# Attention and token/channel mixer in one kernel: load order of the last channel weight, score banks for batch 1's attention products, GpSimd casts of the token weights, and the planner's picking rules

## The chip, the cores and the metric

The kernel runs on one core of one Trainium2 chip. The metric is the device time of one execution in microseconds. Each number given as "the time" is a median over several executions; the profile is one further execution, recorded by the hardware profiler. The core has five instruction queues that matter here: PE (TensorE matrix products), DVE (VectorE), ACT (ScalarE), POOL (GpSimd) and SP (SyncE, which issues every DMA of this kernel). Each works through its own list in order and waits at its head for semaphores.

## What is computed

Eight batches of causal attention with a decay along the sequence, then a mixer: a token product over the sequence and a channel product over the features. Cut to what matters:

```python
batch, n_heads, seq, head_dim = (8, 8, 576, 64)       # d_model 512
d_tok, d_ch = (256, 1536)
...
cum = np.cumsum(np.maximum(s, 0.0), axis=-1)
bias = -(cum[:, :, :, None] - cum[:, :, None, :])
scores = np.where(causal, -1000000000.0, scale * q @ kT + np.minimum(bias, 0.0))
attn = softmax(scores)
x = (attn @ v).transpose(0, 2, 1, 3).reshape(B, S, H * D)
...
xt = x.transpose(0, 2, 1)
h = np.maximum(xt @ w_tok1, 0.0) @ w_tok2
u = x + h.transpose(0, 2, 1)
return u + np.maximum(u @ w_ch1, 0.0) @ w_ch2
```

Inputs and output are float32; the products run in bfloat16 with float32 sums.

## The kernel before

**Work of one batch.** The heads of a batch go in two groups of four (`quad(b, 0)` and `quad(b, 4)`). `stage_qk` loads k and q of four heads (576 KB each), casts them to bfloat16 (`qkb`, L657 on GpSimd, L659 on VectorE, L661 on ScalarE) and VectorE transposes them (L668, `kT` and `qT`). `stage_v` loads v in five chunks and multiplies it with the decay weights (L618, `vp`). `quad` makes scores in two phases (L700, for batches 0 and 1 with a mask product L709), exponentials on ScalarE (L716, tile `E`), for later batches a causal mask on GpSimd (L723), then one set of nine attention products for each head (L740, "AV" below); VectorE takes the reciprocal of the row sums (L749) and normalizes into `x` (L754). `tok` is the token mixer: L964 and L972 (first token weight `w1`), `h` evicted with a relu (L978 ACT, L979 DVE), L989 and L993 (second token weight `w2`), the sum with `x` (L1006), a transpose into `uTa` or `uTb` (by L1019 on TensorE with evictions L1027 and L1029 for batches 0 and 1, by a transposing DMA, L1011, from batch 2 on). `chan` is the channel mixer: L1047 with channel weight 1, relu evictions into `ga` or `gb` (L1053 ACT, L1055 DVE), then L1073 with channel weight 2, the sum L1081 and the store. Batch 0 has its own form of both, `tok0` (L860 with `w1`, L873, L879 with `w2`, evictions L885 and L886) and `chan0` (L902 with channel weight 1, L924 with channel weight 2, L928, copies L935, stores L940).

**PSUM.** There are eight banks: four in the ring `r_sc` (score banks, `psc` in the profile) and four in `r_mx` (mixer banks, `pmx`). Scores of all batches but the first's second phase use `r_sc`. The AV products use `r_mx`, except those of the first four heads of batch 0; so do all products of `tok`, `chan` and `chan0`.

**Weights.** `load_tok1`, `load_tok2` and `load_ch1`, `load_ch2` load the weights in float32 into tiles that are not in use yet (`uTb`, `x`, `ga`, `vf`) and cast them to bfloat16 with `load_w`, whose last argument names the engines that may do the cast (L783 GpSimd, L785 VectorE, L787 ScalarE). Channel weights 1 and 2 come in four groups each (0 to 3) of 768 KB.

**The order of work.** Nothing is written out by hand. Each piece of work is an `Op` with the engines that could do it (and an assumed time on each), what it reads and writes, which ring slots it holds and a priority. `Plan.once` goes through time in a model: for each engine it lists the ops that could start (`cands`), takes those within 0.03 us of the earliest, and picks among them by the longest remaining path (`tail`, from `Plan.tails`) on VectorE, ScalarE and GpSimd, or by priority on TensorE and SP. It may then prefer an op that starts later than the picked one, if that shortens the longer of the two remaining paths; the later op may start as late as the picked one would have ended. An op that another engine could finish sooner is passed over. `Plan.run` repeats this and keeps the shortest plan; the resulting order on each engine is what is emitted. So an edit of one load or one bank can change the order on all engines for the rest of the run. Loads stand in SP's queue in the order of the calls at the end of the kernel (L1095 to L1123): `load_op` chains each load to the one before.

Two more details: the load of k or q needs a free slot of four in `qkf`, which is free when the tile has been cast and, from batch 2 on, squared by ScalarE (L643, a check of the value range). And where TensorE would be idle in the first 45 us of the plan, products of zeros (L1185) are filled in.

Of the kernel before, what the change touches and what calls it, by code (L numbers as in the profile page):

```python
# [49 lines left out]
class Plan:  # L50
# [8 lines left out]
        self.writer = {}  # L59
        self.readers = {}  # L60

    def op(self, alts, reads=(), writes=(), prio=0, dma=0.0, holds=(), after=None, port=False):
        o = Op()
        o.port = port
        o.alts = alts
        o.prio = prio
        o.dma = dma
        o.idx = len(self.ops)
        o.deps = set()
        o.users = []  # L70
        o.bufs = []
        for k in list(reads) + list(writes) + list(holds):
            b = k[0] if isinstance(k, tuple) else k
            if isinstance(b, Buf) and b not in o.bufs:
                o.bufs.append(b)
                b.uses += 1
        for k in reads:
            w = self.writer.get(k)
            if w is not None:
                o.deps.add(w)  # L80
        for k in writes:
            w = self.writer.get(k)
            if w is not None:
                o.deps.add(w)
            for r in self.readers.get(k, ()):
                o.deps.add(r)
        for k in reads:
            self.readers.setdefault(k, []).append(o)
        for k in writes:
            self.writer[k] = o  # L90
            self.readers[k] = []
        o.deps.discard(o)
        o.after = after
        if after is not None:
            o.deps.add(after)
        self.ops.append(o)
        return o
# [12 lines left out]
    def tails(self, order):  # L110
        nxt = {}
        last = {}
        for o in reversed(order):
            nxt[o] = last.get(o.eng)
            last[o.eng] = o
        follow = {}
        for r in {b.ring for o in order for b in o.bufs}:
            prev = {}
            for b in r.uses:
                if b.slot in prev:  # L120
                    for o in prev[b.slot].ops:
                        follow.setdefault(o, []).append(b.ops[0])
                prev[b.slot] = b
        for o in sorted(order, key=lambda o: (-o.start, -o.idx)):
            t = o.fin - o.start
            for u in follow.get(o, ()):
                t = max(t, o.fin - o.start + u.tail)
            for u in o.users:
                t = max(t, self.gap(o, u, o.eng) + u.tail)
            n = nxt[o]  # L130
            if n is not None and o.eng in ("PE", "SP"):
                t = max(t, o.alts[o.eng][0] + n.tail)
            o.tail = t

    def reset(self):
        rings = set()
# [42 lines left out]
    def once(self, use, eps=0.03):  # L179
# [14 lines left out]
        port = 0.0  # L194
# [18 lines left out]
        while left:  # L213
            best = None
            for e in engines:
                lst = []
                tmin = None
                for o in cands[e]:
                    st = slot_time(o)
                    if st is None:  # L220
                        continue
                    est = max(etime[e], o.ready, st)
                    if e == "POOL" or o.port and e == "DVE":
                        est = max(est, port)
                    if use and any(max(etime[x], o.ready, st) + o.alts[x][1] < est + o.alts[e][1] - 0.05
                                   for x in o.alts if x != e):
                        continue
                    lst.append((est, o))
                    if tmin is None or est < tmin:
                        tmin = est  # L230
                if tmin is None:
                    continue
                pick = None
                if use and e in ("DVE", "ACT", "POOL"):
                    for est, o in lst:
                        if est <= tmin + eps:
                            key = (-o.tail, o.idx)
                            if pick is None or key < pick[0]:
                                pick = (key, est, o)
                    for est, o in lst:  # L240
                        _, ep, p = pick
                        if o is p or est > ep + p.alts[e][0]:
                            continue
                        if max(est + o.tail, est + o.alts[e][0] + p.tail) + 0.01 < max(ep + p.tail, ep + p.alts[e][0] + o.tail):
                            pick = (None, est, o)
                else:
                    for est, o in lst:
                        if est <= tmin + eps:
# [191 lines left out]
def kernel(  # L440
# [29 lines left out]
    HQ = 4  # L470
# [94 lines left out]
    def decay():  # L565
        P.op(act(576, lambda: nc.scalar.activation(out=s_sb[:, :], in_=s_sb[:, :], func=AF.Relu)),
             reads=["s"], writes=["sr"], prio=-1)
        P.op({"DVE": (1.3, 1.6, lambda: nc.vector.tensor_tensor_scan(
            out=cum[:, :], data0=one_sb[:, :].to_broadcast([64, S]), data1=s_sb[:, :], initial=0.0, op0=ALU.mult, op1=ALU.add))},
            reads=["sr"], writes=["cum"], prio=-1)  # L570
        P.op(dve(1, lambda: nc.vector.tensor_scalar(
            out=half[:, :], in0=cum[:, S - 1 : S], scalar1=-0.5, scalar2=None, op0=ALU.mult)),
            reads=["cum"], writes=["half"], prio=-1)
        P.op(act(576, lambda: nc.scalar.activation(
            out=wn[:, 0:S], in_=cum[:, :], func=AF.Exp, bias=half[:, 0:1], scale=1.0), True),
            reads=["half", "cum"], writes=["wn"], prio=-1)
        bw = Buf(r_sc, False)

        def w_tr():
            for jc in range(NJ):  # L580
                nc.tensor.transpose(out=bw.t[:, jc * 64 : jc * 64 + 64], in_=wn[:, jc * 128 : jc * 128 + 128],
                                    identity=identf[:, :])
        P.op({"PE": (0.7, 1.1, w_tr)}, reads=["wn"], writes=[(bw, 0)], prio=(0,))
        P.op(dve(320, lambda: nc.vector.tensor_copy(
            out=wT[:, :, :].rearrange("p c e -> p (c e)"), in_=bw.t[:, 0:320])),
            reads=[(bw, 0)], writes=["wT"], prio=-1)
# [92 lines left out]
            square(f, b, h, i)  # L679

    xbuf = {}

    def quad(b, h):
        np_ = (b * H + h) / 2
# [2 lines left out]
        for ph, blocks in enumerate(PHASES):  # L687
# [26 lines left out]
            for e in range(HQ):  # L714
                def ex(p=ps[e], e=e, ph=ph):
                    nc.scalar.activation(out=E.t[:, e, ph * 512 : ph * 512 + 512], in_=p.t[:, :], func=AF.Exp, scale=0.125)  # L716
                P.op(act(512, ex), reads=[(ps[e], 0)], writes=[(E, ph, e)], prio=0)
            if pem:
                continue
            for (jc, a, z) in blocks:  # L720
# [8 lines left out]
        x, vp = xbuf[b], vbuf[b]  # L729
        vkeys = [(vp, c) for c in range(NJ)] + [(vp, "w")]  # L730
        for hh in range(HQ):
            pa, rc = Buf(r_sc if b == 0 and h == 0 else r_mx, False), Buf(r_rc, False)

            def av(pa=pa, hh=hh):
                o = pa.t[:, 0 : NJ * 66].rearrange("p (c n) -> p c n", n=66)
                for ic in range(NJ):
                    j_lo = max(ic - 1, 0)
                    for jc in range(j_lo, ic + 1):
                        d0 = EB[jc] + 128 * (ic - jc)
                        nc.tensor.matmul(out=o[:, ic, 0 : D + 1], lhsT=E.t[:, hh, d0 : d0 + 128],  # L740
                                         rhs=vp.t[:, jc, h + hh, 0 : D + 1], start=(jc == j_lo), stop=(jc == ic))
            P.op({"PE": (9 * 0.035, 9 * 0.035 + 0.3, av)},
                 reads=([(E, ph, hh) for ph in range(2)] if pem else
                        [(E, "m", jc) for jc in range(NJ)]) + vkeys, writes=[(pa, 0)],
                 holds=[x, rc], prio=(np_ if b else -1 + h / 8, 0))
# [48 lines left out]
    def load_tok1(buf):  # L794
        def d1(st):
# [3 lines left out]
        load_w(buf, 0, 5 * DT, d1, lambda st: [  # L799
            [(w1[:, 0:2, :].rearrange("p c n -> p (c n)"), st[:, 0 : 2 * DT])],  # L800
            [(w1[:, 2:4, :].rearrange("p c n -> p (c n)"), st[:, 2 * DT : 4 * DT]),
             (w1[0:64, 4, :], st[0:64, 4 * DT : 5 * DT])]], [("w1", 0), ("w1", 1)], 2.5, ("POOL", "DVE"))
        P.op({"POOL": (0.3, 0.5, lambda: nc.gpsimd.tensor_copy(out=w1[64:128, NJ - 1, 128:256], in_=w1[0:64, NJ - 1, 128:256]))},
             reads=[("w1", 1)], writes=["w1s"], prio=30)

    def load_tok2(buf):
        def d2(st):
            nc.sync.dma_start(out=st.rearrange("p (c n) -> p c n", c=NTC),
                              in_=moe_w_tok2.rearrange("(c p) n -> p c n", p=128))
        load_w(buf, 0, NTC * S, d2, lambda st: [[(w2[:, :, :].rearrange("p c n -> p (c n)"), st)]], ["w2"], 1.5,  # L810
               ("POOL", "DVE"))

    NG = 4
    CG = NCC // NG
# [72 lines left out]
                     reads=[(pt, 1)], writes=[(uT, m, a)], prio=0)  # L887
        return uT

    def chan0(uT):  # L890
        rank = 4 + LAG
        g = Buf(r_gb)
        for c0 in range(0, NCC, CG):
            pms = [Buf(r_mx, False) for _ in range(CG)]
            ms = [[m] for m in range(NMC)] if c0 == 0 else [list(range(NMC))]
            for ml in ms:
                for i in range(CG):
                    cc, pm = c0 + i, pms[i]

                    def mm(cc=cc, pm=pm, ml=ml):  # L900
                        for m in ml:
# [4 lines left out]
                         reads=[(uT, m, a) for m in ml for a in (0, NQ // 2)] +  # L906
                               ([("wc1", 0, m // 2) for m in ml] if c0 == 0 else [("wc1", cc // CG)]) +
                               ([(pm, 0)] if ml[0] else []),
                         writes=[(pm, 0)], holds=[g], prio=(rank + 2.0 * c0 / NCC - 4 * (c0 == 0), 3 + ml[0]))
            for i in range(CG):  # L910
                cc, pm = c0 + i, pms[i]
                P.op(either(512,
# [186 lines left out]
    stage_v(0)  # L1099
    for h in range(0, H, HQ):  # L1100
        quad(0, h)
    load_tok1(Buf(r_uTb))
    load_tok2(Buf(r_x))
    sga, sv = Buf(r_ga), Buf(r_vf)
# [3 lines left out]
    load_ch1(sga, 0, 3)  # L1108
    stage_qk(1, 0)
    load_ch2(sga, 1536, 0)  # L1110
    load_ch2(sv, 0, 1)
    load_ch2(sga, 0, 2)
    load_ch2(sga, 1536, 3)
    stage_qk(1, HQ)
    stage_v(1)
    for b in range(2, B):
        for h in range(0, H, HQ):
            stage_qk(b, h)
# [5 lines left out]
    for b in range(B):  # L1124
# [3 lines left out]
        if b:  # L1128
            chan(b, *tok(b))
        else:  # L1130
            chan0(tok0())

    P.op({"DVE": (1.3, 1.6, lambda: nc.vector.tensor_tensor_scan(
        out=pre[:, :], data0=one_sb[:, :].to_broadcast([64, S]), data1=wn[:, 0:S], initial=0.0, op0=ALU.mult, op1=ALU.add))},
# [99 lines left out]
```

## Time and profile before

| what | value |
|---|---|
| time, median of 6 executions | 297.37 us (296.5 to 298.45) |
| time of the profiled execution | 299.43 us |
| span of the profiled execution | 297.7 us |
| PE busy | 282.8 us, 95% of the span |
| ACT busy | 190.0 us, 64% |
| DVE busy | 169.3 us, 57% |
| POOL busy | 88.3 us, 30% |
| DMA, share of 16 engines, SP's queue | 64.5% |
| granted TensorE clock, mean | 0.989 |

The span is the time from the first to the last instruction in the trace; the execution's own time is a little longer. In the slices of the span each digit is the busy share of 1/40 of it in tenths (9 is 90% or more), and the row PEclk is the clock that TensorE was granted, in tenths of full speed. A line of the list of waits names the waiting engine with tile and line, who released it, the sum in us, how often, and the longest. A line in order of time gives start, length, engine, line, operation, tiles written and read, sizes, how many instructions, and in brackets the idle time before it and what ended it. A row of windows gives the stretch, its length, the busy time of the five engines (matrix products and weight loads of TensorE apart) with the count of instructions, the granted clock, the share of the DMA engines and GB/s.

### The profile page before, as it was taken

What the parts mean: (1) busy time and instruction counts of PE and PEld (TensorE: products, weight loads), DVE (VectorE), ACT (ScalarE), POOL (GpSimd) and SP (SyncE); (2) the same over time, 40 slices, a digit from 0 to 9 for tenths busy, and PEclk for the clock granted to TensorE, in tenths of its full rate; (3) what the DMA queues carried; (4) which work ended last, traced back from release to release, by engine and by line L of the source; (5) the groups of instructions that cost most, each with busy time, mean ns of one, the idle gap of its engine ahead of it and who ended that gap; (6) DMA issues with size and microseconds to landing.
All of it is one profiled execution on the core that took longest, in us unless ns stands there. A gap on an engine that the chain in (4) does not pass through costs nothing.

```text
span 297.7 us, 6653 instructions
## 1 busy us (share of the span) xinstructions
PE 282.8 (95%) x2596; PEld 156.7 (53%) x2596; DVE 169.3 (57%) x326; ACT 190.0 (64%) x359; POOL 88.3 (30%) x133
## 2 busy tenths in 40 slices
PE   8789999688979989999999999999999999999994
PEld 3465455536655534545774545446754545447643
DVE  3984846769686757487644745396425533440022
ACT  3784957669879947856888649985883245107600
POOL 3325002567565503263272213731201301000000
PEclk9999999959999999999999999999999999999999
DMA  7999999998988994976890666756002410151023
GB/s 230 272 343 334 375 309 259 203 353 233 325 188 276 263 218 187 206 184 156 279 203 17 142 250 240 235 111 205 2 0 52 127 73 0 46 116 70 2 72 110
DMA packets 68050, 54.09 MB, mean 182 GB/s; under 512 B 53680, under 2 KB 56560, under 8 KB 68016
## 3 DMA queue, kind: packets, MB, share of 16 engines
q1 hardware_dynamic: 68016, 53.64, 64.5%
q8 instruction: 21, 0.34, 0.5%
q14 instruction: 13, 0.11, 0.1%
HBM read 40.65 MB, written 9.44 MB: 168 GB/s over the span
## 4 chain that ended last, share of the span: by engine, by line
PE 66%; DMA 20%; SPq 6%; DVE 3%; POOL 2%; ACT 1%; issue 1%; DVEq 0%; ACTq 0%; POOLq 0%
PE pmx L1073 26%; PE pmx L1047 24%; DMA qkf<-in_q_dram 10%; DMA ga<-in_moe_w_ch_dram 6%; PE psc L700 4%; PE pmx L740 4%; PE pmx L964 4%; PE pmx L989 4%; SPq L611 3%; DMA vf<-in_v_dram 3%; SPq L638 1%; DMA uTa<-ua 1%; DVE x L754 1%; POOL vp L618 1%; PE pmx L972 1%
## 5 line engine op out<-in xcount | busy, mean ns | idle before, releaser
L716 ACT ACTIVATE E<-psc 128x512 bf16<-128x512 f32 x120 | 63.3, 602 | 22.4 <-PE psc L700 16.9
L1047 PEld LDWEIGHTS <-wc 128*128 128x128 bf16 x528 | 50.7, 98 | 35.0 <-issue 4.7
L723 POOL TENSOR_SCALAR_AFFINE_SELECT E<-E 128x512 bf16<-128x512 bf16 (+1 forms) x60 | 35.1, 615 | 91.9 <-ACT E L716 74.9
L1047 PE MATMUL pmx<-uTb,wc 128*128 128x320 bf16 x384 | 54.0, 299 | 1.8 <-DVE gb L1055 1.5
L1073 PE MATMUL pmx<-wc,gb 128*128 128x512 bf16 (+1 forms) x252 | 54.2, 369 | 0.0
L1053 ACT ACTIVATE gb<-pmx 128x320 bf16<-128x320 f32 x83 | 36.3, 438 | 25.0 <-PE pmx L1047 17.9
L643 ACT ACTIVATE junk<-qkf 128x1152 bf16<-128x1152 f32 x32 | 37.5, 1171 | 10.4 <-DMA qkf<-in_k_dram 8.4
L618 POOL TENSOR_TENSOR vp<-vf,wT 128x512 bf16<-128x512 f32 (+1 forms) x31 | 32.1, 1061 | 17.1 <-PE pmx L740 13.3
L1073 PEld LDWEIGHTS <-gb 128*128 128x128 bf16 x252 | 23.7, 98 | 25.3 <-issue 0.7
L1047 PE MATMUL pmx<-uTa,wc 128*128 128x512 bf16 x144 | 32.6, 379 | 1.3 <-DMA uTa<-ua 1.2
L1073 PE MATMUL pmx<-wc,ga 128*128 128x512 bf16 x144 | 32.6, 379 | 0.0
L754 DVE TENSOR_TENSOR x<-pmx,rc 128x320 bf16<-128x320 f32 x60 | 29.1, 490 | 1.8
L1053 ACT ACTIVATE ga<-pmx 128x512 bf16<-128x512 f32 x29 | 16.9, 603 | 13.1 <-PE pmx L1047 13.1
L740 PEld LDWEIGHTS <-E 128*128 128x128 bf16 x576 | 20.5, 97 | 6.6 <-issue 2.7
L1081 DVE TENSOR_TENSOR of<-pmx,ub 128x512 f32<-128x512 f32 (+1 forms) x17 | 11.2, 661 | 20.6 <-PE pmx L1073 18.7
L668 DVE STREAM_TRANSPOSE kT<-qkb 128x576 f32<-128x576 f32 x16 | 20.0, 1252 | 4.0 <-PE psc L700 3.7
L700 PE MATMUL psc<-qT,kT 32*128 32x256 bf16 (+2 forms) x592 | 19.7, 256 | 2.7 <-DVE rc L749 1.4
L740 PE MATMUL pmx<-vp,E 128*128 128x65 bf16 x540 | 21.3, 193 | 1.0 <-DVE x L754 0.8
L1073 PEld LDWEIGHTS <-ga 128*128 128x128 bf16 x144 | 13.4, 98 | 16.1 <-issue 1.1
L657 POOL CAST qkb<-qkf 128x1152 bf16<-128x1152 f32 (+1 forms) x10 | 10.1, 1010 | 38.0 <-DMA qkf<-in_q_dram 19.6
L700 PEld LDWEIGHTS <-kT 32*128 32x128 bf16 x640 | 13.8, 94 | 12.2 <-issue 9.2
L668 DVE STREAM_TRANSPOSE qT<-qkb 128x576 f32<-128x576 f32 x16 | 19.9, 1243 | 0.3 <-POOL qkb L657 0.3
(109 smaller groups left out, 281.1 us busy)
## 6 DMA issues: line engine op xcount, KB each, us to landing
qkf<-in_k_dram SPq DMA_DIRECT2D x20, 576.0 KB, 5.7
qkf<-in_q_dram SPq DMA_DIRECT2D x20, 576.0 KB, 5.3
vf<-in_v_dram SPq DMA_DIRECT2D x32, 256.0 KB, 6.2
out_dram<-of SPq DMA_DIRECT2D x31, 256.0 KB, 2.4
ga<-in_moe_w_ch_dram SPq DMA_DIRECT2D x6, 768.0 KB, 7.8
vf<-in_moe_w_ch_dram SPq DMA_DIRECT2D x2, 768.0 KB, 9.4
out_dram<-of SPq DMA_DIRECT2D x10, 128.0 KB, 2.7
vf<-in_v_dram SPq DMA_DIRECT2D x8, 128.0 KB, 5.1
```

What stands on the lines that cost most here:

```text
L618: eng.tensor_tensor(out=vp.t[0:n, c, :, 0:D], in0=vf.t[0:n, c, :, :], in1=wT[0:n, c, b * H : b * H + H].unsqueeze(2).to_broadcast([n, H, D ...
L643: P.op({"ACT": (1.1, 1.5, lambda: nc.scalar.activation(out=junk[:, :], in_=f.t[:, :], func=AF.Square, accum_out=sq[:, col : col + 1]))}, r ...
L668: nc.vector.transpose(out=T.t[:, 0:S, :].rearrange("p s q -> p (s q)").bitcast(FP32).rearrange("p (t r) -> p r t", r=R), in_=t1.t[:, :].bi ...
L700: nc.tensor.matmul(out=ps[e].t[:, c0 : c0 + z - a], lhsT=kT.t[p0 : p0 + TP, jc * 128 : jc * 128 + 128, qq], rhs=qT.t[p0 : p0 + TP, a:z, qq ...
L716: nc.scalar.activation(out=E.t[:, e, ph * 512 : ph * 512 + 512], in_=p.t[:, :], func=AF.Exp, scale=0.125)
L723: nc.gpsimd.affine_select(out=w, in_=w, compare_op=ALU.is_ge, fill=0.0, base=0, pattern=[[0, HQ], [1, n]], channel_multiplier=-1)
L740: nc.tensor.matmul(out=o[:, ic, 0 : D + 1], lhsT=E.t[:, hh, d0 : d0 + 128], rhs=vp.t[:, jc, h + hh, 0 : D + 1], start=(jc == j_lo), stop=( ...
L754: nc.vector.tensor_tensor(out=x.t[:, :, (h + hh) * D : (h + hh + 1) * D], in0=o[:, :, 0:D], in1=rc.t[:, :].unsqueeze(2).to_broadcast([128, ...
L964: nc.tensor.matmul(out=pms[t].t[:, :], lhsT=w(0, 128, c, t), rhs=x.t[:, c, :], start=(c == 0), stop=False)
L1047: nc.tensor.matmul(out=pm.t[:, 0 : e - a], lhsT=wc1[:, m, cc * 128 : cc * 128 + 128], rhs=uT.t[:, m, a:e], start=(m == 0), stop=(m == NMC ...
L1053: lambda cc=cc, pm=pm, a=a, e=e: nc.scalar.activation(out=g.t[:, cc, a:e], in_=pm.t[:, 0 : e - a], func=AF.Relu),
L1073: nc.tensor.matmul(out=pm.t[:, na:nb], lhsT=g.t[:, cc, c * 128 : c * 128 + 128], rhs=wc2[:, cc, na:nb], start=(cc == 0), stop=(cc == NCC - 1))
```

## The change

Six edits in one diff:

- In the order of loads, k and q of batch 1's second four heads come ahead of groups 1 and 2 of channel weight 2, and v of batch 1 ahead of group 3, which was ahead of all of them.
- The AV products of batch 1 use the score banks (`r_sc`) instead of the mixer banks.
- The casts of `w1` and `w2` may be done by GpSimd only; VectorE was allowed too.
- The picking rule of the planner: a later op is preferred only if it starts within 0.4 us (or the picked op's own length, if that is shorter); and when an op is passed over because another engine would finish it sooner, the port that GpSimd and VectorE share is now counted for that other engine.
- An op can be given a `lead`, which lengthens its remaining path in the planner: 12 us for the exponential of the decay, and some 2 to 8 us for the exponentials of batch 0.
- The first product of `chan0` has to follow the last AV of batch 0.

```diff
-    def op(self, alts, reads=(), writes=(), prio=0, dma=0.0, holds=(), after=None, port=False):
+    def op(self, alts, reads=(), writes=(), prio=0, dma=0.0, holds=(), after=None, port=False, lead=0.0):
         o = Op()
+        o.lead = lead
...
-            o.tail = t
+            o.tail = t + o.lead
...
-                    if use and any(max(etime[x], o.ready, st) + o.alts[x][1] < est + o.alts[e][1] - 0.05
+                    if use and any(max(etime[x], o.ready, st, port if x == "POOL" or o.port and x == "DVE" else 0.0)
+                                   + o.alts[x][1] < est + o.alts[e][1] - 0.05
                                    for x in o.alts if x != e):
...
-                        if o is p or est > ep + p.alts[e][0]:
+                        if o is p or est > ep + min(0.4, p.alts[e][0]):
...
-            reads=["half", "cum"], writes=["wn"], prio=-1)
+            reads=["half", "cum"], writes=["wn"], prio=-1, lead=12.0)
...
-                P.op(act(512, ex), reads=[(ps[e], 0)], writes=[(E, ph, e)], prio=0)
+                P.op(act(512, ex), reads=[(ps[e], 0)], writes=[(E, ph, e)], prio=0,
+                     lead=8.0 - 2 * ph - h - 0.1 * e if b == 0 else 0.0)
...
-            pa, rc = Buf(r_sc if b == 0 and h == 0 else r_mx, False), Buf(r_rc, False)
+            pa, rc = Buf(r_sc if b == 0 and h == 0 or b == 1 else r_mx, False), Buf(r_rc, False)
...
-            P.op({"PE": (9 * 0.035, 9 * 0.035 + 0.3, av)},
+            lastav[0] = P.op({"PE": (9 * 0.035, 9 * 0.035 + 0.3, av)},
...
-             (w1[0:64, 4, :], st[0:64, 4 * DT : 5 * DT])]], [("w1", 0), ("w1", 1)], 2.5, ("POOL", "DVE"))
+             (w1[0:64, 4, :], st[0:64, 4 * DT : 5 * DT])]], [("w1", 0), ("w1", 1)], 2.5, ("POOL",))
...
-               ("POOL", "DVE"))
+               ("POOL",))
...
-                         writes=[(pm, 0)], holds=[g], prio=(rank + 2.0 * c0 / NCC - 4 * (c0 == 0), 3 + ml[0]))
+                         writes=[(pm, 0)], holds=[g], prio=(rank + 2.0 * c0 / NCC - 4 * (c0 == 0), 3 + ml[0]),
+                         after=None if c0 or ml[0] else av0)
...
     for h in range(0, H, HQ):
         quad(0, h)
+    av0 = lastav[0]
...
     stage_qk(1, 0)
     load_ch2(sga, 1536, 0)
+    stage_qk(1, HQ)
     load_ch2(sv, 0, 1)
     load_ch2(sga, 0, 2)
+    stage_v(1)
     load_ch2(sga, 1536, 3)
-    stage_qk(1, HQ)
-    stage_v(1)
```

The instruction lists of the two built programs show what the planner makes of it. TensorE's list differs from about the first tenth on. Around batch 1 it was: scores, L924, three AVs, scores, one AV, L924, four AVs, scores of batch 2, L964. It is now: scores, L924, scores, L924, three AVs, three of L924, four AVs, three of L924, one AV, nine of L924, L964. The 36 AV products of batch 2's first four heads, which stood between the two runs of L1019, now stand behind the first forty products of L1047. SP's list differs in the loads named above, in the mixing of loads with the stores of batch 0, and in the place of the transposing DMAs, which now follow each other in fours.

More of the change, by code (lines that the diff above doesn't have):

```diff
@@ L681 @@
     xbuf = {}
+    lastav = [None]
     def quad(b, h):
@@ L888, in tok0, with chan0 @@
         return uT
-    def chan0(uT):
+    def chan0(uT, av0):
         rank = 4 + LAG
@@ L1130 @@
         else:
-            chan0(tok0())
+            chan0(tok0(), av0)
     P.op({"DVE": (1.3, 1.6, lambda: nc.vector.tensor_tensor_scan(
```

## The prediction

> **What bounds the kernel now.** I read the slices of the span first, then TensorE's list of waits, then the order of time around the longest of them. The slices (40 of 7.44 us each):
>
> ```profile
> PE   8789999688979989999999999999999999999994
> ...
> PEclk9999999959999999999999999999999999999999
> DMA  7999999998988994976890666756002410151023
> ```
>
> From slice 16 on (about 119 us) PE stands at 9 without a break until the tail: the rest of the run is TensorE work back to back, and no edit here removes any of it. So time can only come from before that. DMA is nearly full up to about 110 us. One slice, 59.5 to 67 us, has PEclk 5. TensorE's waits between 50 and 112 us:
>
> ```profile
> PE pmx L1047 <- DVE gb L1055: 1.5, 1, 1.5
> PE psc L700 <- DVE rc L749: 1.4, 1, 1.4
> PE pmx L964 <- DVE x L754: 1.2, 1, 1.2
> PE pmx L1047 <- DMA uTa<-ua: 1.2, 1, 1.2
> PE pmx L740 <- DVE x L754: 0.8, 2, 0.6
> ```
>
> With two of 0.2 us they make 6.6 us; idle time after 20 us that no wait is named for adds some tenths. All are single events, so I looked at each in order of time. The first cluster (start, length, engine, line):
>
> ```profile
> 55.83 0.43 PE L740 MATMUL pmx<-vp,E 128*128 128x65 bf16 x9 [0.61 <-DVE x L754]
> 56.46 0.79 PE L740 MATMUL pmx<-vp,E 128*128 128x65 bf16 x18 [0.20 <-DVE x L754]
> 58.70 0.74 PE L700 MATMUL psc<-qT,kT 32*128 32x256 bf16 x16 [1.45 <-DVE rc L749]
> 60.68 3.57 PE L964 MATMUL pmx<-x,w 128*128 128x512 bf16 x8 [1.23 <-DVE x L754]
> ```
>
> The reader is to see that TensorE has nothing between batch 1's last attention products (L740) and its mixer (L964) but one score group, while VectorE normalizes six heads with a cast and two transposes among them. And x8 of L964 takes 3.57 us here; the same eight take 1.89 us at 92.56. The clock says why (window; busy PE, PEld, DVE, ACT, POOL; clock; DMA):
>
> ```profile
> 57.00:61.00 4.00, 1.32 (x26) 0.77 (x23) 3.91 (x11) 2.48 (x6) 3.13 (x4) 0.76 1.05 206
> 61.00:65.00 4.00, 4.00 (x18) 1.23 (x20) 1.57 (x3) 1.91 (x5) 1.80 (x4) 0.50 1.00 371
> ...
> 84.00:88.00 4.00, 2.46 (x20) 1.65 (x17) 3.14 (x8) 2.08 (x5) 2.72 (x4) 1.00 0.68 153
> ```
>
> After 2.68 us idle in 4 the clock is at half until about 65.6 us. From 60.68 to 67.61 TensorE does L964, L972, 24 of L700 and L989, 6.93 us; at full clock the same take 2.14 (92.56 to 94.70) + 0.57 (97.40 to 97.97) + 1.73 (128.46 to 130.19 in the chain of waits) = 4.44. The half clock costs **2.5 us**.
>
> **Part by part.** The instruction lists of both built programs give the new order; durations are the trace's, landings are the trace's, shifted by what is moved.
>
> *SP's order.* k and q of batch 1's second half go ahead of groups 1 and 2 of channel weight 2, batch 1's v ahead of group 3. Landings before (first consumer's start): group 0 34.7, groups 1 to 3 36.8, 38.8, 40.9, k 43.5, q 45.0, v 46.1 to 50.7. A weight group takes 2.05 us of the stream, a k or q 1.6, v 5.2. Moved: k 36.3, q 37.9, group 1 39.9, group 2 42.0, v 43.2 to 48, group 3 49.4 to 50.7; nothing more is moved in all. VectorE casts (0.96 each) make them usable at 41, 43 and 50.4 to 51.7. I add TensorE's new order from 36.4 us, where it stands as before: scores 1.1, L902 1.7, L924 and L928 0.9, scores 1.2, L924 with group 0 0.9: 42.2, where group 1 is first read (ready 41). Six with it 1.3, three more with L928 0.9, scores 1.1: 45.5, group 2 (43); 12 L924 2.6, scores 1.2, 0.9, 0.65: 50.8, v (48.8). AV products 0.8: 51.6, group 3. Each is ready about when it is asked for, the last with the least room (0 to 1 us). Cost 0; from outside −0.2 to +1.0.
>
> *Score banks for batch 1's attention products.* The mixer banks stay with L924, so the three L924 groups with weight group 3 can stand among and behind the AV products: nine of L924 (1.95 us) now follow the last AV. My sum brings the last AV to 54.4, the ninth L924 to 56.3. VectorE now has only reciprocals and norms there (eight pairs of 0.11 + 0.49, from 51.1, stretched by the AVs): last norm 56.1. L964 starts at 56.3 instead of 60.68, with one score group (0.56) still to do. The transposes behind the norms (2.4 us) end at 58.6: L700 waits 0.3, L989 0.3 for h behind them. The cluster of 3.5 us becomes 0.6: **−2.9**. What is queued behind an AV that waits for a score bank is all of TensorE; the bank is given back by the exponentials of the second score group (ACT, 0.5 each, from 48.9), done by 51, before need. The half clock goes too: **−2.5**.
>
> Here the Trainium skill bears on the sum: "TensorE: Matmul & The Clock Gate", Part 1, has the half clock follow an idle window of about 3.4 us. By that, single gaps of 1.45 and 1.23 us with work between them should not cool the array; the trace shows they did, when idle time filled two thirds of 4 us, and that 1.54 us idle of 4 (the 84 us row) did not. The trace decides. In the new order the worst stretch (next item) is 1.6 idle of 4, near the harmless row, so I take no half clock; by the other reading it stays at 2.5, kept for the range.
>
> *What is late next.* Between the L1019 transposes and L1047 the 36 AVs of batch 2 are no longer there as cover (they come later in TensorE's order). VectorE does four adds (0.62), one eviction, two adds (0.69), three evictions in a row, and ACT's eviction L1027 now stands behind a cast of q of batch 2 (landing 63.9 by my shift, 64.9 before). I get L1047 at 65.5 with 1.6 us idle since 62.5, against 0.6 before: **+1.0** (0 to +2).
>
> *66 to 110 us.* Before: 1.54 idle at 86.5, where VectorE's L1055 stood behind a cast that waited for q of batch 4; that cast is elsewhere now. New: 24 score matmuls behind ACT's exponentials at 72.2, 0.5; two L1055 behind the cast of k of batch 3 (about 78.3 against 80.6 before; cast 0.95, transpose 1.25, eviction 0.45) where TensorE wants the bank at 80.1, 0.7. Together **−0.3** (−1.5 to +3). The 1.22 us for uTa at 109.9: the four transposing DMAs now follow each other in SP's queue, ahead of the stores and most of v of batch 5, but compete with loads that SP issues late, because squares free their slots late (ACT, 74.8 and 79.8): I take half, **−0.6** (−1.2 to +1).
>
> *w1 and w2 cast by GpSimd alone.* Three casts in a row after the landing at 18.8: 0.62 (the 128x512 row), again, 0.40: w1 at 20.4 instead of 20.03; TensorE's L860 waited to 20.09. **+0.3**. Then w2 (128x1152, 1.15 as L657's), done 21.7; first read about 22.5. The Trainium skill speaks against this edit: "GPSIMD Engine Reference", 3 and 8, has elementwise work roughly twice as fast on VectorE, and the SBUF interfaces shared. By that factor on the 0.58 and 0.76 rows w1 would come at 21.5 (+1.4) and w2 at 23 (+0.5 more). The rows say 0.62 beside 0.58 and 1.15 beside 0.76, and VectorE reads PSUM in its norms then; I take the rows, and keep +1.9 as the upper end.
>
> *The rest at 0.* The first GpSimd cast of q lets VectorE transpose k about 0.8 us sooner: hidden, the landing of w1 at 18.7 decides; without that cover it is −0.8. The wait of L902 for the last AV of batch 0 is already met by the order of before. The leads, the 0.4 us limit and the port term act only through the order counted above.
>
> **Sum**: −2.9 − 2.5 + 1.0 − 0.3 − 0.6 + 0.3 = **−5.0 us**. From 110 us on TensorE is full, so the lead stays. The profiled execution has a span of 297.7 and a time of 299.43; it would be 292.7 and 294.4. It lay 2.1 above the median of the six runs (297.37, from 296.5 to 298.45), so the median comes to **292.4**.
>
> **Rivals.**
> 1. *The head of the mixer is freed and most new stalls don't come* (14%). The lists keep the AVs of batch 2 near and the DMA stream keeps ahead. Then most of the 7 us idle and the 2.5 of clock go: about 289.5. For it: VectorE is only 56% busy. Against: DMA is at 9 up to 110 us.
> 2. *DMA supply, not order, holds TensorE: the lead is mostly given back* (16%). If k of batch 3 lands when it did (80.6), its bank comes at 83.2, 3.1 after need: 2.4 more than counted, 294.8; with w1's upper end 296. For it: the stream is full and its bytes are the same. Against: before, SP issued that k only at 72.97.
> 3. *Slower* (12%): the same wait, longer. Behind VectorE's cast of k of batch 3 stand the two evictions; TensorE is idle meanwhile, so the clock halves (2.5). Without this wait and its 0.7 the gain is 5.7; the idle time s plus 2.5 eats that from s = 3.2, a landing after 80.7, and from there each us counts. At 82.5 it is 299. Speaks for it: that is the landing of before. Against: k and q slots are issued earlier now.
> 4. *The change does nothing that decides* (4%): group 3 lands late enough to put the gap where it was, 297.4.
>
> Forecast 54%. Change within 0.3% (0.9 us, about what a measurement can tell from none): 0.06, from rival 4 and the edge of 2. Faster: 0.54 + 0.14 + 0.14 = 0.82. Slower: 0.12. The range that holds 8 of 10, from rival 1 to the edge of 2: 289.0 to 297.0; the unknown costs' ends lie within it, but for several at once.
>
> **What would show it.** L964 near 56 us with L924 right before it; PEclk 9 in the ninth slice; L1047 of batch 1 at 65 to 67 (72.06 before), of batch 2 near 103 to 105 (109.94). I am wrong if PEclk still falls, if L924 waits for weight group 3, or if a wait of over 3 us for L1055 appears near 80 us.

## The result and the profile after

| kernel | median | executions | lowest to highest | ratio to before, 95% interval |
|---|---|---|---|---|
| before | 297.61 us | 67 | 295.60 to 300.06 | |
| after | 294.83 us | 30 | 292.60 to 298.49 | 0.9903 [0.9888, 0.9918] |

The change makes the kernel 2.8 us faster by the medians (1.0%). Forecast were 5.0. The profiled execution of after took 297.98 us and is one of its slowest: in six of 32 executions TensorE had a granted clock of 0.992 to 0.994, and these took 296.7 to 298.5 us.

Lines of the changed file stand up to six further down: L924 is now L929, L964 L969, L1019 L1024, L1047 L1052, L740 L744, L754 L758, L1055 L1060. The clock in the slices (now 7.41 us each):

```profile
PEclk9999999988999999999999999999999999999999
```

In PEclk the 5 of the ninth slice is gone, but the ninth and tenth (59.3 to 74.1 us) have 8: a shorter dip has come, a little later. TensorE's waits from 50 us on, as in the first part of the prediction:

```profile
PE pmx L1052 <- DVE x L758: 1.6, 1, 1.6
...
PE pmx L744 <- DVE gb L1060: 0.6, 1, 0.6
```

None of the waits listed before for the mixer's first product (L964 for `x`, 1.2) or for scores (L700 for `rc`, 1.4) is left. TensorE in order of time, as far as it answers to the lines of before:

```profile
51.16 0.81 PE L929 MATMUL pmx<-wc,gb 128*128 128x512 bf16 x3 [0.37 <-DVE wc L789]
...
54.01 2.10 PE L929 MATMUL pmx<-wc,gb 128*128 128x512 bf16 x9
55.95 1.89 PE L969 MATMUL pmx<-x,w 128*128 128x512 bf16 x8
...
64.11 0.40 PE L1024 MATMUL pmx<-ident,us 128*128 128x128 bf16 x4 [0.94 <-DVE us L1011]
65.53 5.41 PE L1052 MATMUL pmx<-uTb,wc 128*128 128x320 bf16 x28 [1.02 <-ACT uTb L1032]
...
78.09 5.13 PE L1052 MATMUL pmx<-uTb,wc 128*128 128x320 bf16 x36 [1.60 <-DVE x L758]
...
107.12 1.02 PE L1052 MATMUL pmx<-uTa,wc 128*128 128x512 bf16 x4 [1.00 <-DMA uTa<-ua]
```

The mixer starts at 55.95, was 60.68, right behind nine L929, and its first eight products take 1.89 instead of 3.57 us. The line at 51.16 is a short wait for the cast of weight group 3. But the 28 products at 65.53 take 5.41 us, more than x36 of the same shape at 78.09: the half clock now falls there. The rows of windows (stretch, length, busy PE, PEld, DVE, ACT, POOL with counts, clock, DMA, GB/s):

```profile
61.00:65.00 4.00, 2.50 (x48) 1.75 (x45) 3.68 (x8) 2.79 (x5) 2.32 (x3) 1.00 1.00 386
65.00:69.00 4.00, 3.47 (x15) 2.06 (x15) 3.97 (x5) 3.03 (x7) 2.44 (x3) 0.57 1.03 293
```

TensorE is idle 1.50 us in the first four, as much as in the row of before that the prediction took as harmless (1.54 at 84 to 88 us), and here the clock falls.

### The profile page after: what moved, and what is told of

Read it like the earlier page. It is cut to its first block, busy times and chain, and to the rows that moved or that the text cites. A ratio compares the mean times of both kernels' runs of the same rounds, so it can differ in the third digit from the quotient of the medians.

```text
span 296.3 us, 6638 instructions
## 1 busy us (share of the span) xinstructions
PE 282.9 (95%) x2597; PEld 156.6 (53%) x2597; DVE 174.6 (59%) x332; ACT 182.7 (62%) x344; POOL 93.3 (31%) x138
## 4 chain that ended last, share of the span: by engine, by line
PE 69%; DMA 12%; SPq 9%; DVE 5%; ACT 3%; issue 1%; POOL 0%; ACTq 0%
PE pmx L1078 26%; PE pmx L1052 26%; SPq L613 8%; DMA qkf<-in_k_dram 5%; DMA vf<-in_v_dram 4%; PE pmx L744 4%; PE psc L703 4%; PE pmx L969 4%; PE pmx L994 3%; DMA ga<-in_moe_w_ch_dram 2%; ACT E L719 1%; DMA uTa<-ua 1%; DVE x L758 1%; DVE qkb L661 1%; PE pmx L977 1%
## 5 line engine op out<-in xcount | busy, mean ns | idle before, releaser
L1052 PEld LDWEIGHTS <-wc 128*128 128x128 bf16 x528 | 51.1, 99 | 36.4 <-issue 5.4
L1052 PE MATMUL pmx<-uTb,wc 128*128 128x320 bf16 x384 | 55.9, 304 | 2.6 <-DVE x L758 1.6
L1058 ACT ACTIVATE gb<-pmx 128x320 bf16<-128x320 f32 x79 | 34.4, 438 | 27.2 <-PE pmx L1052 19.5
L620 POOL TENSOR_TENSOR vp<-vf,wT 128x512 bf16<-128x512 f32 (+1 forms) x30 | 31.1, 1062 | 9.8 <-PE pmx L744 9.3
L1052 PE MATMUL pmx<-uTa,wc 128*128 128x512 bf16 x144 | 32.8, 379 | 1.0 <-DMA uTa<-ua 1.0
L1078 PE MATMUL pmx<-wc,ga 128*128 128x512 bf16 x144 | 33.4, 379 | 0.0
L659 POOL CAST qkb<-qkf 128x1152 bf16<-128x1152 f32 (+1 forms) x15 | 15.6, 1037 | 36.2 <-DMA qkf<-in_q_dram 14.8
L758 DVE TENSOR_TENSOR x<-pmx,rc 128x320 bf16<-128x320 f32 x52 | 25.5, 490 | 1.7
L744 PEld LDWEIGHTS <-E 128*128 128x128 bf16 x576 | 20.9, 97 | 7.0 <-issue 1.7
L1058 ACT ACTIVATE ga<-pmx 128x512 bf16<-128x512 f32 x24 | 14.4, 599 | 15.4 <-PE pmx L1052 15.4
L703 PE MATMUL psc<-qT,kT 32*128 32x256 bf16 (+2 forms) x592 | 20.3, 251 | 1.0 <-ACT E L719 0.4
L753 DVE RECIPROCAL rc<-pmx 128x5 f32<-128x5 f32 x52 | 9.5, 185 | 16.1 <-PE pmx L744 13.4
```

Of the source, the lines that this page charges most:

```text
L620: eng.tensor_tensor(out=vp.t[0:n, c, :, 0:D], in0=vf.t[0:n, c, :, :], in1=wT[0:n, c, b * H : b * H + H].unsqueeze(2).to_broadcast([n, H, D ...
L703: nc.tensor.matmul(out=ps[e].t[:, c0 : c0 + z - a], lhsT=kT.t[p0 : p0 + TP, jc * 128 : jc * 128 + 128, qq], rhs=qT.t[p0 : p0 + TP, a:z, qq ...
L758: nc.vector.tensor_tensor(out=x.t[:, :, (h + hh) * D : (h + hh + 1) * D], in0=o[:, :, 0:D], in1=rc.t[:, :].unsqueeze(2).to_broadcast([128, ...
L1052: nc.tensor.matmul(out=pm.t[:, 0 : e - a], lhsT=wc1[:, m, cc * 128 : cc * 128 + 128], rhs=uT.t[:, m, a:e], start=(m == 0), stop=(m == NMC ...
L1058: lambda cc=cc, pm=pm, a=a, e=e: nc.scalar.activation(out=g.t[:, cc, a:e], in_=pm.t[:, 0 : e - a], func=AF.Relu),
L1078: nc.tensor.matmul(out=pm.t[:, na:nb], lhsT=g.t[:, cc, c * 128 : c * 128 + 128], rhs=wc2[:, cc, na:nb], start=(cc == 0), stop=(cc == NCC - 1))
```

## The experiments

**The changed kernel again**, for an execution without that half clock.

> The changed kernel unaltered, as the yardstick for the others. If the half clock at 65 us in its profile (5.41 us for 28 products of L1052, against 3.83 at full clock) is a chance of the clock's window, it is absent in most executions: granted clock 0.997 to 1.0 and a profile with L1052 at 65.5 taking 3.9 us. If it belongs to the kernel, it is there again. Time 294.5, ratio 0.990.

Measured: 293.72 us (292.54 to 297.42), ratio 0.9888 [0.9854, 0.9921]. Its profiled execution took 292.88 us at a clock of 1.0; TensorE in order of time, and the same windows:

```profile
53.45 2.10 PE L929 MATMUL pmx<-wc,gb 128*128 128x512 bf16 x9
55.39 1.89 PE L969 MATMUL pmx<-x,w 128*128 128x512 bf16 x8
...
63.55 0.40 PE L1024 MATMUL pmx<-ident,us 128*128 128x128 bf16 x4 [0.94 <-DVE us L1011]
...
74.59 5.13 PE L1052 MATMUL pmx<-uTb,wc 128*128 128x320 bf16 x36 [1.05 <-DVE x L758]
...
102.42 1.02 PE L1052 MATMUL pmx<-uTa,wc 128*128 128x512 bf16 x4 [0.72 <-DMA uTa<-ua]
```

```profile
61.00:65.00 4.00, 2.94 (x52) 2.16 (x41) 3.65 (x8) 3.74 (x8) 2.57 (x4) 1.00 1.03 377
65.00:69.00 4.00, 4.00 (x42) 2.65 (x41) 4.00 (x5) 3.52 (x9) 3.03 (x5) 1.00 1.11 307
```

Same program, same gap of 0.94, but ScalarE's eviction is in time: 1.06 us idle instead of 1.50, and the clock stays. In 11 of these 12 executions it is 0.997 or more. The execution with the half clock is 0.6 us later at L969, 3.5 at 78.09 and 5.2 us longer in span.

**The half clock of before by itself.** Eight products of zeros stand in two of TensorE's gaps ahead of the mixer (0.61 us at 55.8 and 1.45 us at 58.7 in before); nothing else is moved.

```diff
+    for at, n in ((423, 2), (537, 6)):
+        for _ in range(n):
...
+            f.fn = lambda t=r_sc.tiles[0]: nc.tensor.matmul(
+                out=t[:, :], lhsT=zero[:, 0:128], rhs=zero[:, :], start=True, stop=True)
...
```

> The kernel before with eight products of zeros put in where TensorE stood idle (two before the second AV of batch 1's second four heads, six before the first scores of batch 2), nothing else moved. Theory clock: the idle time of 57 to 61 us falls from 2.7 to about 1.3 us, the half clock from 59.5 to 65.6 goes, and the time falls by 2.5 us (ratio 0.992), with no wait removed. Rival: the half clock costs nothing because DMA sets the pace after 66 us; the time stays (0.999 to 1.001), and the wait at 86.5 us grows by as much.

Measured: 296.12 us, ratio 0.9965 [0.9933, 0.9998]: between theory and rival. In its profiled execution (span 293.6, clock 1.0), TensorE in order of time:

```profile
59.40 1.89 PE L964 MATMUL pmx<-x,w 128*128 128x512 bf16 x8 [1.34 <-DVE x L754]
...
63.28 2.11 PE L989 MATMUL pmx<-h,w 128*128 128x512 bf16 x8 [1.10 <-DVE h L979]
...
69.76 3.42 PE L1047 MATMUL pmx<-uTb,wc 128*128 128x320 bf16 x24 [0.24 <-DVE x L754]
...
105.89 1.02 PE L1047 MATMUL pmx<-uTa,wc 128*128 128x512 bf16 x4 [1.15 <-DMA uTa<-ua]
```

The stall stays (1.34), the half clock is gone: eight L964 take 1.89 us. L1047 starts at 69.76 instead of 72.06, but these 2.3 us are not all the clock's. L964 is already 1.28 us sooner, and so is VectorE's cast ahead of the last norms, for which a q landed sooner (the first line is before, the second this run):

```profile
54.62 0.76 DVE L659 CAST qkb<-qkf 128x1152 bf16<-128x1152 f32 x1 [1.56 <-DMA qkf<-in_q_dram]
```

```profile
53.34 0.76 DVE L659 CAST qkb<-qkf 128x1152 bf16<-128x1152 f32 x1 [1.16 <-DMA qkf<-in_q_dram]
...
61.86 0.76 DVE L659 CAST qkb<-qkf 128x1152 bf16<-128x1152 f32 x1 [2.00 <-DMA qkf<-in_k_dram]
62.54 0.68 DVE L979 TENSOR_SCALAR h<-pmx 128x512 bf16<-128x512 f32 x1
```

From L964 to L1047 it is 10.36 us instead of 11.38, so the clock is worth 1.0 us in this execution. The products are faster by more, but TensorE then waits 1.10 us for `h`, which VectorE evicts behind a cast that waits for a k. At the median the clock is worth 1.0 as well (0.1 to 2.0); in nine of the 12 executions it was 0.997 or more, and their median is 295.56, 1.7 below before. Of the 71 executions of before that ran beside the experiments, 70 had 0.980 to 0.994: its half clock is the rule, not an accident of one profile. Against the median of after_again, 296.12 − 293.72 = 2.4 us remain for the order of work.

**The two named edits alone, without the planner's.** Loads as after; banks as after; both.

```diff
     load_ch2(sga, 1536, 0)
+    stage_qk(1, HQ)
     load_ch2(sv, 0, 1)
     load_ch2(sga, 0, 2)
+    stage_v(1)
     load_ch2(sga, 1536, 3)
-    stage_qk(1, HQ)
-    stage_v(1)
...
-            pa, rc = Buf(r_sc if b == 0 and h == 0 else r_mx, False), Buf(r_rc, False)
+            pa, rc = Buf(r_sc if b == 0 and h == 0 or b == 1 else r_mx, False), Buf(r_rc, False)
```

> The kernel before with the order of loads alone; the planner makes its order anew. Theory banks: without the score banks for batch 1's AV the last products of L924 can't stand behind the AV, so the gap before L964 and the half clock stay: time 296.5 to 298 (ratio 0.997 to 1.002). Rival: the order of loads is what moves L924, and the time falls by 2 to 3 us.

> The kernel before with the score banks for batch 1's AV alone. Theory banks: the AV no longer contend with L924 for the mixer banks, and L924 can be put beside them even with weight group 3 ahead of v: 1 to 3 us faster (ratio 0.990 to 0.997). Rival, loads: by the time v of batch 1 is there all of L924 is done, nothing is left as cover before L964, and the time stays or rises.

> The kernel before with the order of loads and the banks, without the planner's edits and with VectorE allowed for w1 and w2. Theory: the two named edits carry the gain, 294 to 295.5 (ratio 0.988 to 0.993), with L964 at 56 us and the clock full there. Rival: the planner's edits carry it, and this is within 1 us of before.

Measured: loads 296.54 us, ratio 0.9961 [0.9926, 0.9995]; banks 299.64, 1.0063 [1.0031, 1.0095]; both 302.74, 1.0141 [1.0094, 1.0187]. Together they do not add up to the gain; they lose 4.8 us. VectorE in order of time with both:

```profile
52.23 0.76 DVE L659 CAST qkb<-qkf 128x1152 bf16<-128x1152 f32 x1 [4.59 <-DMA qkf<-in_k_dram]
...
54.19 0.17 DVE L749 RECIPROCAL rc<-psc 128x5 f32<-128x5 f32 x1
```

VectorE stands 4.59 us at the head of its queue for a k of batch 2; all norms of batch 1, and with them the score banks, are queued behind. This stall alone does not make the 4.8 us, though. With the loads alone the first norm is just as late, behind two such casts, and that run is not slower than before:

```profile
53.49 0.76 DVE L659 CAST qkb<-qkf 128x1152 bf16<-128x1152 f32 x1 [1.54 <-DMA qkf<-in_q_dram]
54.17 0.18 DVE L749 RECIPROCAL rc<-pmx 128x5 f32<-128x5 f32 x1
```

And with both, TensorE reaches batch 2's L1047 at 109.31 us, 0.6 sooner than in the profile before (109.94). In this execution the loss comes behind it:

```profile
109.31 1.02 PE L1047 MATMUL pmx<-uTa,wc 128*128 128x512 bf16 x4 [1.34 <-DMA uTa<-ua]
...
114.94 0.27 PE L700 MATMUL psc<-qT,kT 32*128 32x256 bf16 x1 [1.35 <-ACT E L716]
...
117.34 8.75 PE L1047 MATMUL pmx<-uTa,wc 128*128 128x512 bf16 x28
```

```profile
113.15 1.16 ACT L643 ACTIVATE junk<-qkf 128x1152 bf16<-128x1152 f32 x1 [10.91 <-DMA qkf<-in_k_dram]
```

```profile
118.00:122.00 4.00, 4.00 (x10) 1.32 (x9) 2.55 (x4) 2.73 (x6) 2.34 (x4) 0.50 0.20 31
```

ScalarE waits 10.91 us for a late k and squares it ahead of the exponentials that TensorE needs; TensorE waits 1.35 us, and the clock falls to half. This execution took 305.06 us, 2.3 above the run's median, so the lines show where it lost time, not the whole of the 4.8.

**The GpSimd casts taken back.** The changed kernel, VectorE allowed again for `w1` and `w2`.

```diff
-             (w1[0:64, 4, :], st[0:64, 4 * DT : 5 * DT])]], [("w1", 0), ("w1", 1)], 2.5, ("POOL",))
+             (w1[0:64, 4, :], st[0:64, 4 * DT : 5 * DT])]], [("w1", 0), ("w1", 1)], 2.5, ("POOL", "DVE"))
...
-               ("POOL",))
+               ("POOL", "DVE"))
```

> The changed kernel with VectorE allowed again for the casts of w1 and w2; planned anew. By the rows of the profile GpSimd alone costs 0.1 to 0.3 us at L864 and this is faster by that or the same (ratio to before 0.988 to 0.991). By the skill's factor of two it would be 1 us or more faster. If the new plan is worse elsewhere it shows as a wait after 60 us.

Measured: 294.04 us, ratio 0.9845 [0.9797, 0.9892]. It is not slower than after, so this edit is not what carries the gain.

**The 0.4 us rule.** First the two named edits with this rule and no other edit; then the changed kernel with the rule taken out; then all the planner's edits and the casts without the two named ones.

```diff
-                        if o is p or est > ep + p.alts[e][0]:
+                        if o is p or est > ep + min(0.4, p.alts[e][0]):
```

> The kernel before with the two named edits (loads, score banks) and one more: a later op is preferred only if it starts within 0.4 us. No casts moved, no leads, no port term. With the two named edits alone the time was 302.7 us. In the built order the three groups of channel weight 2 products stand between the last attention products of batch 1 and its mixer, as in the changed kernel. Theory (the 0.4 us rule is what makes the two named edits pay): 294 to 295.5 us, no wait of over 1 us before the mixer's first product. Rival (the GpSimd casts, or all planner edits together, are needed): 298 us or more, with waits of over 1 us for exponentials or score tiles as in the kernel with the two edits alone.

> The changed kernel with the 0.4 us limit taken out again (a later op may start as late as the picked one would have ended); all else stays. Two groups of channel weight 2 products stand behind the last attention products of batch 1 instead of three. Theory (the rule is what makes the named edits pay): 297 us or more, the gain is mostly lost. Rival (loads, banks and casts carry it, the rule only trims): 293.5 to 295.5 us.

> The changed kernel without the two named edits: loads and banks as before; 0.4 us rule, port term, leads and GpSimd casts as after. No group of channel weight 2 products stands behind batch 1's last attention products. Theory (the gain needs loads and banks, which put those products there): 296.5 to 299 us, with the stall before the mixer's first product still of 1 us or more. Rival (the picking rule carries the gain by itself): 294 to 295.5 us.

Measured: named edits and rule 294.44 us, ratio 0.9885 [0.9843, 0.9927]; after without the rule 298.29, 1.0024 [0.9998, 1.005]; planner's edits and casts alone 304.10, 1.0221 [1.0178, 1.0263]. The theory held in the first two; in the third the direction held, but the run is slower than either theory had it. In one table (medians in us):

| | loads and banks as before | as after |
|---|---|---|
| planner and casts as before | 297.6 | 302.7 |
| only the 0.4 us rule added | not run | 294.4 |
| planner and casts as after | 304.1 | 294.8 |

So the named edits and the rule carry the gain together, and the other planner edits and the casts add nothing that is measurable. What the rule does in the plan can be followed in the kernels: with it, the second pass of `Plan.run` is the shortest in the model (286.8 us for after, 287.3 for the named edits and the rule). Without it, every later pass is longer than the first, so the first is kept (288.8 and 289.5), and that one picks by priority or by who is ready first, not by the longest remaining path.

What that does on the chip is seen in part on VectorE. First the changed kernel without the rule, then the changed kernel (second profile), both in order of time:

```profile
51.59 0.96 DVE L789 CAST wc<-ga 128x1536 bf16<-128x1536 f32 x1 [2.74 <-DMA ga<-in_moe_w_ch_dram]
54.62 0.76 DVE L661 CAST qkb<-qkf 128x1152 bf16<-128x1152 f32 x1 [2.06 <-DMA qkf<-in_k_dram]
55.29 0.33 DVE L753 RECIPROCAL rc<-psc 128x5 f32<-128x5 f32 x3
```

```profile
49.60 0.96 DVE L789 CAST wc<-ga 128x1536 bf16<-128x1536 f32 x1 [2.78 <-DMA ga<-in_moe_w_ch_dram]
50.47 0.19 DVE L753 RECIPROCAL rc<-psc 128x5 f32<-128x5 f32 x1
...
51.17 1.15 POOL L659 CAST qkb<-qkf 128x1152 bf16<-128x1152 f32 x1 [13.64 <-DMA qkf<-in_k_dram]
```

In the model this cast can start at 49.4 us in all versions that load as after. Without the rule it goes to VectorE, ahead of the norms; on the chip the k lands later and the norms wait. With the rule it goes to GpSimd. Without the rule L969 starts at 61.00 us, with it at 55.39; how much of this is the cast is not shown, since weight group 3 is also cast 2.0 us later there, and the rest of the plan differs.

That such a cast can hold TensorE is seen one step later in the named edits with the rule, in an execution of 296.71 us, its slowest; TensorE waits for an add (L1006) that stands behind the cast:

```profile
62.57 0.80 DVE L659 CAST qkb<-qkf 128x1152 bf16<-128x1152 f32 x1 [3.11 <-DMA qkf<-in_k_dram]
```

```profile
64.02 0.62 PE L993 MATMUL pmx<-h,w 128*64 128x512 bf16 x4 [2.75 <-DVE ub L1006]
```

The planner's edits alone lose elsewhere: they reach the mixer of batch 2 sooner than before (89.69 us instead of 92.56) and its L1050 on `uTa` 4.0 us later, with two score groups more ahead of it. TensorE's longest wait there, ScalarE and SP in order of time, and the window:

```profile
PE pmx L1050 <- DMA uTa<-ua: 3.3, 1, 3.3
```

```profile
84.47 0.44 ACT L1056 ACTIVATE gb<-pmx 128x320 bf16<-128x320 f32 x1 [2.08 <-PE pmx L1050]
84.80 1.16 ACT L645 ACTIVATE junk<-qkf 128x1152 bf16<-128x1152 f32 x1
...
86.56 0.32 SPq L640 DMA_DIRECT2D qkf<-in_k_dram  x1
```

```profile
81.00:85.00 4.00, 2.19 (x17) 1.45 (x16) 3.93 (x8) 1.81 (x5) 2.06 (x4) 1.00 0.00 0
```

DMA is at 0.00: SP cannot issue the next k until ScalarE has squared an earlier tile; the square stands behind an eviction that waits 2.08 us for TensorE, which itself waits for VectorE. The reader is to see a stall that goes round by three engines. That the 3.3 us for `uTa`, 30 us later, come from this empty stretch of the DMA queue is likely, but no run tried it.

**The stalls left in after.** Three runs move single ops in the changed kernel by setting their planned start (one `MOVE` line each): the scan and checks of the value range some 50 us later; ScalarE's cast of q of batch 2 behind the eviction L1032; and eight ops, so that the adds for the last 64 rows, which L1024 waits for, come behind two evictions, and 320-column products come ahead of them.

```diff
+    MOVE = {1365: 120.0, 1366: 120.1}
+    MOVE = {153: 61.9}
+    MOVE = {153: 61.9, 449: 60.91, 453: 61.17, 455: 61.18, 457: 63.3, 467: 63.6, 458: 63.61, 150: 63.65}
+    for o in order:
+        o.start = MOVE.get(o.idx, o.start)
```

> The changed kernel, order kept, but the scan and the value checks (L1139 to L1149) are moved 50 us later on VectorE. Theory port: these small instructions wait for GpSimd (1.52 us for three on one element, 0.26 before; 0.91 for the copy, 0.16 before) and stand in front of the norms for which L1052 waits 1.6 us at 78; that wait goes, and the time falls by 1.3 to 1.6 us against the changed kernel (ratio to before 0.985). Rival, masks and supply: the AV are late because of the masks or the load of k of batch 3, so that the wait moves to 84 us (now 0.65) and the time falls by under 0.5 us.

> The changed kernel, order kept, but ScalarE's cast of q of batch 2 (L663) comes behind the eviction L1032 instead of ahead of it. Theory head of the queue: L1032 ends 1.05 us sooner, TensorE's L1052 starts at 64.6 instead of 65.5, idle time before it is 0.1 instead of 1.0 us, and the time falls by 0.9 us (ratio to before 0.987); executions with the half clock become rarer. Rival: VectorE's evictions end just as late (64.5 and 64.8), so L1052 gains 0.3 us or less and the time stays.

> The changed kernel with eight ops moved by hand around batch 1's channel mixer: ScalarE's cast of q of batch 2 behind its eviction of a transposed tile, VectorE's evictions of the second and third tile ahead of the two adds for the last 64 rows, and the transposes of those rows behind the first two groups of channel weight 1 products (which read only the first 320 columns). In the changed kernel TensorE waits 0.94 us there for these adds. Theory (that wait is on the path): it falls to 0.3 us or less and the time to 292.5 to 293.2 us. Rival (the wait is given back at the next one, the transposing DMA or VectorE's cast of k of batch 3): 293.5 to 294.5 us, no difference from the changed kernel.

Measured: checks late 294.46 us, ratio 0.9901 [0.9858, 0.9944]; cast behind 293.47, 0.9883 [0.9846, 0.992]; products first 295.72, 0.9931 [0.9903, 0.9958]. None is shown to be faster than after, and products first is slower than theory and rival had it. With the checks late, the wait of L1052 for `x` is gone from the list, and a new one stands in it:

```profile
PE pmx L744 <- DVE of L1086: 0.9, 1, 0.9
```

Batch 2's L1052 on `uTa` starts 1.2 us sooner than in after_again (101.23 instead of 102.42), but from there to the end this run takes 1.8 us longer. The new wait, at 130 us, comes behind the moved scan and checks, which now delay VectorE from 122.9 to 125.1 us.

With products first, TensorE in order of time:

```profile
63.62 1.25 PE L1052 MATMUL pmx<-uTb,wc 128*128 128x320 bf16 x8 [0.62 <-ACT uTb L1032]
...
65.98 2.88 PE L1052 MATMUL pmx<-uTb,wc 128*128 128x320 bf16 x20 [0.75 <-ACT gb L1058]
```

The 0.94 for the adds became 0.62 and 0.75: the third group of products now needs a bank that ScalarE has not emptied. In all three, closing a gap of about 1 us ahead of 80 us did not shorten the kernel, as the rivals had it. No version ran that is shown to be faster than after.

## Why the prediction was right, and where it was off

- **Direction, bound and place: right.** L969 at 55.4 to 56.0 us (56.3 forecast), nine L929 in front of it; the `x` and `rc` waits of the first cluster are gone.
- **The stall at the transposes, +1.0: right.** L1052 starts at 64.0 to 65.5 us (65.5 forecast), and 0.9 to 2.0 us are idle there (1.6).
- **66 to 110 us, −0.3 − 0.6: right in the undisturbed execution.** TensorE is idle some 1.9 us there, 2.8 before (1.8 forecast), and L1052 on `uTa` starts at 102.4 (103 to 105). In the execution with the half clock it is idle 3.4 us. The wait for `x` (1.05 and 1.60) was not forecast. VectorE's eviction behind the cast of k of batch 3 cost at most 0.6, where rival 3 saw the danger.
- **`w1` and `w2` on GpSimd: too high by 0.2.** The first L864 starts at 20.15 us in the profile of after, L860 at 20.09 before; after_casts shows no cost at all. The factor of two was the wrong reading, as taken.
- **The largest miss: "the half clock goes too: −2.5".** It does go: the granted clock is 0.997 or more in 26 of the 32 executions of after, and below that in nearly all of before. But it is worth 1.0, not 2.5. The prediction added up by how much the products from L964 to L989 are longer, and took it that all of this is on the path. before_warm shows what stands behind it: at full clock TensorE comes to L989 before `h` is ready and waits 1.10 us. That holds within one execution and at the median alike.
- **"From 110 us on TensorE is full, so the lead stays": not quite.** From batch 2's first product on `uTa` on, the same 1556 products are left in all four profiles. They and the tail behind them take 187.8 us in before and before_warm, 188.7 and 189.1 in the two of after. So 0.9 to 1.4 us of the lead are lost, where the prediction put nothing. No wait there is longer than 0.22 us; it is spread over many small differences, and their cause stays open.
- **That the rest agrees is in part luck.** With 1.0 for the clock the forecast would be −3.5 (measured −2.8). The other terms sum to −2.5, and the medians of before_warm and after_again differ by 2.4; but the loss behind 110 us is in the 2.4 and not in the sum.
- **"1.54 idle of 4 did not" was no safe side.** After itself loses the clock in some executions, with 1.50 idle of 4. One row of one execution was too little for a limit. The Trainium skill ("TensorE: Matmul & The Clock Gate", Part 1) says that the activity window runs freely, so that the same kernel meets it in another phase each time. That would fit one program with both outcomes; no run here sets the phase.
- **Of the three signs of being wrong, two came, both small.** PEclk falls in six of 32 executions, and L929 waits 0.37 us for weight group 3. The wait of over 3 us near 80 us did not come.
- **What the parts are worth by themselves** the prediction did not ask. It put the gain on loads and banks and said that the 0.4 us rule acts through the order. That is so, but without the rule there is no such order, and the same two edits cost 1.4%. The leads and the tie of `chan0` to the last AV change nothing: built without the one or the other, each engine's list of instructions is the same as after.
- **Rival 2 and 3** (k of batch 3 late) did not come: VectorE casts it at 76.3 us in the undisturbed execution, 79.8 in the other, before the 80.6 from which they count. (Rival 1 takes VectorE as 56% busy; the page has 57%.)

## What to carry to other kernels

An order made by a planner is only as good as the landing times it assumes: an in-order engine that holds a cast for a load at its head makes all behind it as late as that load. Whether that costs time depends on who needs what stands behind: in one run VectorE's wait of 3.11 us became 2.75 us on TensorE; in another, norms held up by two such casts left the kernel no slower than before. Edits to loads, to banks and to the picking rule have to be judged together; each half alone lost 1.4 to 2.2% where both gained 1%. And a stretch at half clock is not worth what its products are longer by: look for what TensorE would wait for if it came through sooner.

## What the hardware did that was not expected

Some VectorE instructions take longer while GpSimd is busy. First before, then after, both in order of time on VectorE:

```profile
89.46 0.26 DVE L1140 SCALAR_TENSOR_TENSOR gap<-wn,s_sb 64x1 f32<-64x1 f32 x3
...
89.82 0.16 DVE L1143 COPY bad<-gap 64x4 f32<-64x4 f32 x1
```

```profile
74.88 1.52 DVE L1146 SCALAR_TENSOR_TENSOR gap<-wn,s_sb 64x1 f32<-64x1 f32 x3
...
76.50 0.91 DVE L1149 COPY bad<-gap 64x4 f32<-64x4 f32 x1
...
79.77 2.43 DVE L661 CAST qkb<-qkf 128x1152 bf16<-128x1152 f32 x1
```

Three instructions of one element per partition take 1.52 instead of 0.26 us, a copy of four 0.91 instead of 0.16, a cast 2.43 where the same shape took 0.76. GpSimd has a mask or a product with v in progress nearly all the time from 74.2 to 81.6 us; at 89.5 in before it was idle. In the run with the checks late the same instructions stand at 124.7 us, with GpSimd idle from 123.4 to 126.5, and take 0.29 and 0.16 us. The norms between them, which read PSUM, keep their 0.49. The Trainium skill ("GPSIMD Engine Reference", 8) has GpSimd share its SBUF interfaces with VectorE instructions that have two SBUF inputs or a two-port mode, which fits; it puts no number on it. No run changed GpSimd's work alone, so the cause is likely, not shown.
